# The first seven attention tiles written out by hand, and keys loaded whole from the fourth batch on

## The chip, the cores and the metric

The kernel runs on one core of a Trainium2 chip. The metric is the device time of one execution in microseconds (us). The engines are PE (matrix products), DVE (vector), ACT (scalar functions and copies), POOL (general) and SP, whose queue issues most transfers. Each works through its own instructions in order and waits on semaphores for the others.

## The reference

Three stages, each feeding the next. The inputs of the first are q, k and v of 8 batches, 8 heads, 576 positions and 64 dimensions.

```
k_p = mean of k over groups of 8 positions      # 72 pooled keys per head
v_p = mean of v over groups of 8 positions
attn = softmax(q @ k_p^T / 8)                   # per batch and head
x    = attn @ v_p                               # 4608 tokens x 512

expert = argmax over 8 experts of cos(x, expert_emb) / tau
x = gate * (relu(x @ w1[expert]) @ w2[expert])  # one expert of 8 per token

h   = max(x @ m1, x @ m2, x @ m3)               # 512 x 768 each
out = h @ m_out
```

## The kernel before, in words

The schedule is written by hand: the order of the Python calls is the order of the instructions on each engine. The attention stage handles 36 tiles of 128 tokens (4.5 per batch; tiles 4, 13, 22 and 31 hold half of one batch and half of the next), followed by the experts' products (`ph`, `py`), whose token gathers begin before the last tiles are done, and the third stage (`p`, `o`).

For one tile i there are five steps: `stage_q` transposes the queries on PE (tile `pqT`) and ACT copies them out; `stage_s` multiplies them with the pooled keys (`psc`), and DVE takes the maximum (`mx`) and subtracts it (`sh`); `stage_e` is the exponential on ACT; `stage_a` transposes the weights on PE (`paT`), two ACT copies follow (`aT`); `stage_x` multiplies with the pooled values (`pav`), and DVE scales by the reciprocal sum (`rs`, `x`), forms the expert scores (`dt`, `lg`), and SP stores x. A square sum on ACT (`sq`) is put off to a list, `squares`. Tiles 0 and 1, 2 and 3 and so on share one weights buffer, as each of the two computes four heads for both; so `stage_a(0)` needs the exponentials of tiles 0 and 1.

The loop (line 1607) runs these steps interleaved: iteration `it` calls `stage_s(it-1)`, `stage_a(it-3)`, `stage_q(it)`, `stage_e(it-1)`, the squares, `stage_x(it-4)`, then the jobs listed in `todo[it]`. PE's order is thus scores, weights transpose, query transpose, weighted values, each of another tile.

Keys and values of a batch are prepared by `prep_steps(b)` (line 297): pooling (sums of 8 rows) on DVE by one reduction per chunk (`pool_k`, `pool_v1`), or on POOL by three halvings per chunk (`pool_k2`, `pool_v`); there are five chunks of rows, four of 128 and one of 72. Then `dup_k` (ACT), transposes on PE (`ptk`, `ptv`), copies into the block-diagonal keys `kbd` (ACT), `spread_v` (POOL), and `vdot`: ten narrow matmuls (`pd`) of values with expert directions, and one DVE product. The list `at_` says at which iteration each step of a batch runs. Batches 0 to 2 are loaded whole (`load_rows`); from batch 3 on half of each row is loaded (`load_half`) and POOL later issues a transfer that adds the other half on top (`add_half`), so that pooling needs two halvings instead of three. Raw rows have two buffers each for k and v. The expert norm (`en_steps`) and constants (`const_steps`) are short DVE steps that `fill` takes from a queue between the steps of a tile.

PSUM has two rotating banks `pq` and one double bank each with the tags `psc`, `paT` and `pav`.

Of the kernel before, what the change touches and what calls it, by code (L numbers as in the profile page):

```python
# [8 lines left out]
F32 = mybir.dt.float32  # L9
# [12 lines left out]
def attention_moe_moe_kernel(  # L22
# [24 lines left out]
    nc = tc.nc  # L47
# [72 lines left out]
    if True:  # L120
# [61 lines left out]
        if True:  # L182
# [31 lines left out]
            def load_rows(pool_tag, src, b, sizes, apart=False, step=4):  # L214
                t = kvp.tile([P, 5, J, D], F32, tag=pool_tag, name=f"{pool_tag}{b}")
# [76 lines left out]
            for i in range(3):  # L292
                if i > 0:
                    nc.gpsimd.memset(kbds[i], 0.0)
                nc.gpsimd.tensor_scalar(vbds[i][:, :, D : D + 1], mslot, float(J), None, A.mult)

            def prep_steps(b):
# [9 lines left out]
                def pool_all():  # L307
                    for c in range(5):
                        pool_k(c)
# [21 lines left out]
                def spread_v():  # L331
                    for c, (h0, h1) in enumerate(HS):
# [7 lines left out]
                        )  # L340

# [67 lines left out]
                if b == 2:  # L409
                    pk = [lambda: (pool_k(0), pool_v(0, 4, P), pool_v(4, 5, R4)), *(lambda c=c: pool_k(c) for c in range(1, 5))]  # L410
# [23 lines left out]
            def stage_q(i):  # L434
# [11 lines left out]
                nc.scalar.copy(qT, ps.rearrange("p (c n) -> p c n", n=P))  # L446
                st_q[i] = qT

            def stage_s(i):
                m, part, t, segs = tiles[i]  # L450
                qT = st_q.pop(i)
                ps = pb.tile([P, 2, 512], F32, tag="psc", name=f"psc{i}")
# [63 lines left out]
            def stage_x(i):  # L516
                m, part, t, segs = tiles[i]
                aT = st_a.pop(i)
                ps = pb.tile([P, 2, 512], F32, tag="pav", name=f"pav{i}")
# [53 lines left out]

            uses = {}

            def uname(name):
                uses[name] = uses.get(name, 0) + 1
                return f"{name}_{uses[name]}"
# [926 lines left out]
            p0[0]()  # L1505
            def en_steps():
                en2 = yield from inverse_norm(ap1, ess, E, 1, "en")
                vs(en, en, en2[:, 0:1], A.mult)
                yield
                ps = pq.tile([P, 512], F32, tag="pq", name="pe0")  # L1510
# [3 lines left out]

            tok_i = rp.tile([P, NT], I32, name="tok_i")
# [71 lines left out]
            queue.append([chain(en_steps())])  # L1587
            p0[1]()
            todo = {0: [lambda: fill(16), p0[2]], 1: [lambda: fill(2), p0[3]], 2: [p0[4]], 3: [p0[5]], 5: [lambda: queue.append([chain(const_steps())])]}
# [12 lines left out]
            qnext = 3  # L1602
            kvnext = 2
# [3 lines left out]
            for it in range(NT + 4):  # L1607
# [13 lines left out]
                while qnext < len(qorder) and qorder[qnext][0] * 9 + qneed[qorder[qnext][1]] - 4 <= it:  # L1621
                    load_q(*qorder[qnext])
                    qnext += 1
                while kvnext < B and kvnext * 4.5 - 11 <= it:
                    if kvnext < NFULL:
                        kv[kvnext] = (load_rows("kraw", k, kvnext, RC), load_rows("vraw", v, kvnext, RC))
                    else:
                        kv[kvnext] = (load_half("kraw", k, kvnext), load_half("vraw", v, kvnext))
                    kvnext += 1
# [18 lines left out]
                for job in todo.get(it, []):  # L1648
                    if callable(job):
                        job()  # L1650
                        continue
                    b, j = job
                    if b not in cur:
                        cur[b] = prep_steps(b)
                    cur[b][j]()
# [351 lines left out]
```

## Time and profile before

| | |
|---|---|
| median of 3 runs | 1204.89 us (1204.51 to 1204.91) |
| profiled execution | 1203.55 us |
| its span, first to last instruction | 1201.4 us |
| PE busy | 1175.2 us (98%) |
| DVE busy | 873.2 us (73%) |
| ACT busy | 606.8 us (51%) |
| POOL busy | 297.4 us (25%) |
| granted TensorE clock, mean over the span | 0.997 |

A line of the timeline gives an instruction's start, its duration (of the whole run of xN instructions, first start to last end), engine, line in the kernel, operation, what it writes and reads, shape and count; in brackets the engine's idle time before it and what ended it. Ends of matmuls include the latency of the pipeline, so that neighbours overlap in the list.

### The profile page before, as it was taken

To read this page: it belongs to the slowest core of one execution; us is meant where nothing else is said; L and a number is where in the kernel's file an instruction comes from. 1 tells how busy PE (TensorE), PEld (TensorE's weight loads), DVE (VectorE), ACT (ScalarE), POOL (GpSimd) and SP (SyncE) were. 2 spreads that over 40 slices of the span, in tenths; PEclk is the share of its full clock that TensorE was granted. 3 is DMA by queue.
4 is the path that set the end of the run, shared out by engine and by line. 5 is a ranking of instruction groups with operands and counts; after the bars stand their busy time and mean duration, and the time that the engine had idled before them with its cause. 6 is when DMAs were issued, how large, how long until landed. Compare 5 with 4: busy or idle time off the path is not lost.

```text
span 1201.4 us, 23859 instructions
## 1 busy us (share of the span) xinstructions
PE 1175.2 (98%) x8761; PEld 1161.6 (97%) x8761; DVE 873.2 (73%) x1811; ACT 606.8 (51%) x1118; POOL 297.4 (25%) x462
## 2 busy tenths in 40 slices
PE   5999999999999999999999999999999999999997
PEld 4899999999999999999999999999999999999997
DVE  6878977978799999988765468468467557567563
ACT  4667674545666666666655244334334334334332
POOL 7978634001222122221201301103104004004001
PEclk9999999999999999999999999999999999999999
DMA  9899656328874457554939668877878877878873
GB/s 294 238 270 253 175 172 220 111 21 239 268 251 177 153 176 238 200 206 135 345 110 323 231 252 302 302 263 290 318 258 287 307 271 281 298 287 284 287 258 141
DMA packets 108121, 285.11 MB, mean 237 GB/s; under 512 B 17879, under 2 KB 70565, under 8 KB 97629
## 3 DMA queue, kind: packets, MB, share of 16 engines
q1 hardware_dynamic: 87436, 216.40, 51.8%
q0 software_dynamic: 20560, 67.11, 17.9%
q8 instruction: 71, 1.16, 0.4%
q14 instruction: 54, 0.43, 0.1%
HBM read 285.52 MB, written 52.48 MB: 281 GB/s over the span
## 4 chain that ended last, share of the span: by engine, by line
PE 92%; DVE 3%; ACT 2%; issue 1%; POOL 0%; DMA 0%; SPq 0%; POOLq 0%; DVEq 0%; ACTq 0%
PE p L1752 33%; PE ph L1097 17%; PE py L1158 17%; PE o L1864 10%; PE pav L524 3%; PE psc L470 2%; PE ph L1105 2%; PE py L1142 2%; PE px L1051 1%; PE paT L501 1%; PE pqT L445 1%; DVE sh L488 1%; DVE kp L305 1%; PE pd L379 1%; POOL out_dram L1872 0%
## 5 line engine op out<-in xcount | busy, mean ns | idle before, releaser
L1752 PE MATMUL p<-yhi,wt 128*128 128x384 f32 x1512 | 387.4, 336 | 0.1
L1752 PEld LDWEIGHTS p<-yhi,wt 128*128 128x128 f32 x1512 | 273.4, 188 | 0.3 <-issue 0.3
L1752 PE MATMUL p<-ylo,wt 128*128 128x384 f32 x756 | 254.1, 336 | 0.0
L1760 ACT COPY s<-p 128x384 f32<-128x384 f32 x162 | 77.6, 479 | 200.7 <-PE p L1752 200.7
L1158 PE MATMUL py<-hhi,whi 128*128 128x256 f32 x576 | 164.6, 286 | 0.0
L1097 PE MATMUL ph<-xhi,wlo 128*128 128x256 f32 x576 | 163.1, 283 | 0.5 <-DVE wlo L1077 0.5
L1097 PE MATMUL ph<-xhi,whi 128*128 128x256 f32 x576 | 163.5, 284 | 0.0
L1097 PE MATMUL ph<-xlo,whi 128*128 128x256 f32 x576 | 163.0, 283 | 0.0
L1158 PE MATMUL py<-hhi,wlo 128*128 128x256 f32 x576 | 162.9, 283 | 0.0
L1158 PE MATMUL py<-hlo,whi 128*128 128x256 f32 x576 | 162.9, 283 | 0.0
L1752 PEld LDWEIGHTS p<-ylo,wt 128*128 128x128 f32 x756 | 142.2, 188 | 0.0
L1864 PE MATMUL o<-wt,ghi 128*128 128x256 f32 x756 | 136.2, 282 | 0.0
L1779 DVE TENSOR_TENSOR blk<-p,s 128x384 f32<-128x384 f32 x108 | 59.6, 552 | 88.8 <-PE p L1752 88.8
L1737 POOL DMA_INDIRECT gt<-gbuf,ix x26 | 33.9, 1304 | 337.9 <-DMA ix<-idbuf 267.9
L1864 PEld LDWEIGHTS o<-wt,ghi 128*128 128x128 f32 x756 | 116.7, 188 | 0.9 <-DVE m L1780 0.8
L1097 PEld LDWEIGHTS ph<-xhi,wlo 128*128 128x128 f32 x576 | 110.5, 192 | 0.7 <-DVE wlo L1077 0.7
L1097 PEld LDWEIGHTS ph<-xhi,whi 128*128 128x128 f32 x576 | 110.5, 192 | 0.0
L1097 PEld LDWEIGHTS ph<-xlo,whi 128*128 128x128 f32 x576 | 110.5, 192 | 0.0
L1158 PEld LDWEIGHTS py<-hlo,whi 128*128 128x128 f32 x576 | 110.5, 192 | 0.0
L1158 PEld LDWEIGHTS py<-hhi,whi 128*128 128x128 f32 x576 | 110.4, 192 | 0.0
L1158 PEld LDWEIGHTS py<-hhi,wlo 128*128 128x128 f32 x576 | 110.4, 192 | 0.0
L1077 DVE TENSOR_TENSOR wlo<-w2raw,whi 128x1024 fp32r<-128x1024 f32 x86 | 105.1, 1225 | 6.9 <-ACT whi L1068 6.8
(345 smaller groups left out, 2348.6 us busy)
## 6 DMA issues: line engine op xcount, KB each, us to landing
wt<-wdram SPq DMA_DIRECT2D x69, 1792.0 KB
w1raw<-in_moe_w_dram SPq DMA_DIRECT2D x88, 512.0 KB
w2raw<-in_moe_w_dram SPq DMA_DIRECT2D x88, 512.0 KB
wdram<-wst POOLq DMA_DIRECT2D x9, 1792.0 KB, 6.6
ybuf<-yo SPq DMA_DIRECT2D x40, 256.0 KB
cvraw<-in_moe_w_dram POOLq DMA_DIRECT2D x36, 256.0 KB, 4.4
xbuf<-x SPq DMA_DIRECT2D x16, 512.0 KB
yr<-ybuf SPq DMA_DIRECT2D x20, 384.0 KB
```

The lines of the kernel that those rows point to most:

```text
L470: nc.tensor.matmul(ps[:, c // 2, (c % 2) * 2 * SP : (c % 2 + 1) * 2 * SP], qT[:, c, :], kbds[segs[0][2] % 3][:, h0 + c].rearrange("p t s - ...
L524: nc.tensor.matmul(ps[lo:hi, bank, (g0 % 4) * DA : (g0 % 4 + g1 - g0) * DA], aT[:, c, lo:hi], vbds[b % 3][:, sl : sl + g1 - g0, :].rearran ...
L1077: nc.vector.tensor_tensor(lo, src, hi.bitcast(F32), op=A.subtract)
L1097: nc.tensor.matmul(ps[:, f, :], a_[:, c, fs], b_[:, c, :], start=(n == 0), stop=(n == 3 * DC - 1))
L1105: nc.tensor.matmul(ps[:, f, 0:P], tl["w1"][piece][:, c, fs], xlo[:, c, 0:P], start=(c == 0), stop=(c == DC - 1))
L1142: nc.tensor.matmul(ps[h], a_[:, f, 0:P], b_[:, f, cols], start=(piece == 0 and f == 0 and n == 0), stop=(last_ and f == 1 and n == 2),)
L1158: nc.tensor.matmul(py[:, c // 2, (c % 2) * 256 : (c % 2 + 1) * 256], a_[:, f, c * P : (c + 1) * P], b_[:, f, :], start=(piece == 0 and f = ...
L1737: nc.gpsimd.indirect_dma_start(out=gt[g][:, j : j + 1], out_offset=None, in_=gbuf[:, :], in_offset=bass.IndirectOffsetOnAxis(ap=cols[j], a ...
L1752: nc.tensor.matmul(ps, a_, b_, start=(start and c + n == 0), stop=(c == 1 and n == 2), skip_group_check=True)
L1760: nc.scalar.copy(t, ps)
L1779: tt(src, add[0], add[1], op=A.add)
L1864: nc.tensor.matmul(ps, a_, b_, start=(m in (1, 2, 5) and c + n == 0), stop=(c == KH - 1 and n == 2), skip_group_check=True,)
```

## The change

Buffers of raw rows get a tag per parity of the batch, one buffer each. Keys are loaded whole in every batch, so POOL's pooling of keys always takes three halvings; values from batch 3 on still come by halves. Loads of batch 1 move up by one query load. Before the first keys come, `turn(22)` issues 22 products of the identity with itself, and `turn(3)` and `turn(12)` stand later; their result is not used. Two chunks of batch 0's keys go from DVE to POOL, and the expert norm runs on DVE between the other three. The iterations 0 to 7 of the loop are replaced by a list of calls, with scores of tiles 0 to 2 in other PSUM tags; the loop begins at iteration 8. Steps of batch 2 move to iterations 8 to 10, the pooling of batch 3 from iteration 6 to 9, the constants from 5 to 11.

```
             def load_rows(pool_tag, src, b, sizes, apart=False, step=4):
-                t = kvp.tile([P, 5, J, D], F32, tag=pool_tag, name=f"{pool_tag}{b}")
+                t = kvp.tile([P, 5, J, D], F32, tag=f"{pool_tag}{b % 2}", name=f"{pool_tag}{b}_", bufs=1)
...
+            kv[1] = [load_rows("kraw", k, 1, RC)]
             load_q(0, 1)
-            kv[1] = [load_rows("kraw", k, 1, RC)]
+            kv[1].append(load_rows("vraw", v, 1, RC))
             load_q(0, 2)
-            kv[1].append(load_rows("vraw", v, 1, RC))
...
+            def later_blocks(i0, i1):
+                for i in range(i0, i1):
                     nc.gpsimd.memset(kbds[i], 0.0)
+                    nc.gpsimd.tensor_scalar(vbds[i][:, :, D : D + 1], mslot, float(J), None, A.mult)
+            def turn(n):
+                ps = pb.tile([P, 2, 512], F32, tag="pav", name=uname("turn"))
+                for _ in range(n):
+                    nc.tensor.matmul(ps[:, 0, 0:P], ident, ident, start=True, stop=True)
...
-                def pool_all():
-                    for c in range(5):
+                def pool_one(c):
+                    n = RC[c]
+                    for w in (4, 2, 1):
+                        dst = kt[0:n, c, 0:w, :] if w > 1 else kp[0:n, c, 0:1, :]
+                        nc.gpsimd.tensor_tensor(dst, kt[0:n, c, 0:w, :], kt[0:n, c, w : 2 * w, :], op=A.add)
+                def pool_all(between):
+                    pool_one(1)
+                    pool_one(4)
+                    for c, n in ((0, 5), (2, 11), (3, 0)):
+                        for _ in range(n):
+                            next(between, None)
                         pool_k(c)
...
-                        for w in (4, 2, 1) if b < NFULL else (2, 1):
+                        for w in (4, 2, 1):
...
+                def trans_k0():
+                    for tag, c0, c1, h0, h1 in (("paT", 0, 4, 0, 7), ("psc", 4, 5, 7, 8)):
...
                 if b == 0:
                     return [
-                        lambda: (pool_all(), dup_k(), trans_k(range(4), 0, 7), trans_k([4], 7, 8)),
-                        lambda: (pool_v(2, 4, P), pool_v(4, 5, R4)),
-                        lambda: pool_v1(0),
-                        lambda: (pool_v1(1), spread_v()),
+                        lambda between: (pool_all(between), dup_k(), trans_k0()),
+                        lambda: pool_v(2, 4, P),
+                        lambda: (pool_v1(0), pool_v1(1), pool_v1(4), spread_v((2, 3, 0, 1, 4))),
                         lambda: (trans_v(0, 4), trans_v(4, 5)),
-                        lambda: vdot(),
+                        vdot,
                     ]
                 if b == 1:
                     return [
-                        lambda: (pool_k(0), pool_k(1), pool_k2(RC, 2), pool_v(0, 4, P), pool_v(4, 5, R4)),
-                        lambda: (dup_k(), spread_v(), trans_k(range(4), 0, 7), trans_k([4], 7, 8)),
+                        lambda: (pool_k(0), pool_k(1)),
+                        lambda: (pool_k2(RC, 2), pool_v(0, 4, P), pool_v(4, 5, R4), spread_v()),
+                        dup_k,
+                        lambda: (trans_k(range(4), 0, 7), trans_k([4], 7, 8)),
                         lambda: (trans_v(4, 5), trans_v(0, 4)),
                         vdot,
                     ]
                 if b == 2:
-                    pk = [lambda: (pool_k(0), pool_v(0, 4, P), pool_v(4, 5, R4)), *(lambda c=c: pool_k(c) for c in range(1, 5))]
+                    pk = [lambda: (pool_v(0, 4, P), pool_v(4, 5, R4))]
+                    pk += [lambda c0=c0: [pool_k(c) for c in range(c0, min(c0 + 2, 5))] for c0 in (0, 2, 4)]
                     return pk + [spread_v, lambda: trans_kv(range(4), 0), lambda: trans_kv([4], 4 * P), vdot]
...
-                at_ = {1: [2, 4, 6, 7], 2: [5, 6, 6, 7, 7, 7, 8, 9, 10]}.get(b, at_[:4] + at_[5:6])
+                at_ = {1: [], 2: [None, None, 8, 8, 9, 9, 9, 10], 3: [9, 10, 12, 13, 14]}.get(b, at_[:4] + at_[5:6])
                 if b >= NFULL:
-                    todo.setdefault(need - 9, []).append(
-                        lambda b=b: (add_half(k, b, kv[b][0]), add_half(v, b, kv[b][1]))
+                    todo.setdefault(8 if b == 3 else need - 9, []).append(
+                        lambda b=b: add_half(v, b, kv[b][1])
                     )
...
+            turn(22)
+            en_left = en_steps()
+            p0[0](en_left)
...
+            later_blocks(1, 2)
             p0[1]()
...
+            load_kv(2)
+            for _ in en_left:
+                pass
+            stage_q(0)
+            stage_q(2)
+            turn(3)
+            stage_s(0)
+            stage_s(2)
+            en_products()
+            p0[2]()
+            later_blocks(2, 3)
+            turn(12)
+            stage_e(0)
+            stage_e(2)
+            stage_q(1)
+            stage_q(3)
+            stage_s(1)
+            p0[3]()
+            stage_s(3)
+            stage_e(1)
+            p0[4]()
+            stage_a(0)
+            stage_e(3)
+            p1 = prep_steps(1)
+            p1[0]()
+            p1[1]()
+            stage_x(0)
+            stage_a(1)
+            stage_x(1)
+            stage_q(4)
+            stage_a(2)
+            p1[2]()
+            p1[3]()
+            stage_x(2)
+            kv[3] = [load_rows("kraw", k, 3, RC)]
+            load_q(1, 0)
+            stage_a(3)
+            stage_s(4)
+            stage_q(5)
+            sq_rest()
+            stage_x(3)
+            stage_s(5)
+            stage_e(4)
+            sq_rest()
+            stage_a(4)
+            stage_q(6)
+            cur[2] = prep_steps(2)
+            cur[2][1]()
+            kv[3].append(load_half("vraw", v, 3))
+            stage_s(6)
+            stage_e(5)
+            p1[4]()
+            cur[2][0]()
+            p1[5]()
+            stage_q(7)
+            stage_e(6)
+            for it in range(8, NT + 4):
```

## Rows read from the trace of the kernel before

**Rows 1.** The page's engines: busy us, share of the span, instructions.
```profile
PE 1175.2 (98%) x8761; PEld 1161.6 (97%) x8761; DVE 873.2 (73%) x1811; ACT 606.8 (51%) x1118; POOL 297.4 (25%) x462
```
**Rows 2.** The chain of waits that ended last, share of the span by engine.
```profile
PE 92%; DVE 3%; ACT 2%; issue 1%; POOL 0%; DMA 0%; SPq 0%; POOLq 0%; DVEq 0%; ACTq 0%
```
**Rows 3.** Timeline, the start: start us, us, engine, line, operation, count, idle before.
```profile
7.37 2.88 DVE L305 TENSOR_REDUCE kp<-kraw 128x64 f32<-128x512 f32 x3 [1.25 <-DMA kraw<-in_k_dram]
...
9.89 1.19 PE L347 MATMUL ptk<-ident,kp 128*128 128x128 f32 x5 [9.89 <-ACT kp L323]
```
**Rows 4.** Timeline of PE, first tiles.
```profile
12.27 1.11 PE L445 MATMUL pqT<-ident,qgrp 128*128 128x128 f32 x4 [1.19 <-ACT kbd L352]
...
18.65 2.29 PE L470 MATMUL psc<-kbd,qT 128*128 128x144 f32 x8 [0.67 <-ACT qT L446]
...
22.72 1.15 PE L470 MATMUL psc<-kbd,qT 128*128 128x144 f32 x8
```
**Rows 5.** Timeline of PE, later: one of each kind, and the waits.
```profile
23.71 0.71 PE L501 MATMUL paT<-ident,at 128*128 128x128 f32 x5
24.25 0.60 PE L445 MATMUL pqT<-ident,qgrp 128*128 128x128 f32 x4
24.69 1.18 PE L379 MATMUL pd<-enT,vT 128*128 128x16 f32 x10
...
28.17 1.69 PE L524 MATMUL pav<-vbd,aT 128*128 128x146 f32 x12
...
32.00 1.19 PE L456 MATMUL psc<-kbd,qT 128*64 128x144 f32 x14 [0.79 <-ACT kbd L352]
...
46.20 1.95 PE L470 MATMUL psc<-kbd,qT 128*128 128x144 f32 x8 [1.05 <-DVE sh L488]
...
56.27 1.25 PE L470 MATMUL psc<-kbd,qT 128*128 128x144 f32 x8 [0.29 <-ACT qT L446]
```
**Rows 6.** Busy time by stretch: PE, PEld, DVE, ACT, POOL, granted clock, DMA share, GB/s.
```profile
46.00:48.00 2.00, 1.80 (x9) 1.82 (x10) 2.00 (x12) 1.30 (x3) 1.76 (x5) 0.63 1.22 199
```
**Rows 7.** Timeline of all engines: steps of DVE and ACT around a tile.
```profile
28.25 0.76 DVE L488 TENSOR_TENSOR sh<-psc,mx 128x576 f32<-128x576 f32 x1
...
29.64 0.55 ACT L323 COPY kp<-kp 128x256 f32<-128x256 f32 x2
...
35.88 0.17 DVE L534 TENSOR_SCALAR rs<-pav 128x8 f32<-128x8 f32 x1 [1.02 <-PE pav L524]
...
37.18 0.28 DVE L551 TENSOR_REDUCE lg<-dt 128x8 f32<-128x64 f32 x1
...
37.51 0.58 ACT L503 COPY aT<-paT 128x512 f32<-128x512 f32 x1 [1.11 <-PE paT L501]
...
37.99 0.26 ACT L504 COPY aT<-paT 72x128 f32<-72x128 f32 x1
38.15 0.59 ACT L446 COPY qT<-pqT 128x512 f32<-128x512 f32 x1
...
48.50 1.98 DVE L305 TENSOR_REDUCE kp<-kraw 128x64 f32<-128x512 f32 x2
...
52.04 0.68 ACT L494 ACTIVATE at<-sh 128x576 f32<-128x576 f32 x1 [1.34 <-DVE sh L488]
...
52.63 0.61 ACT L557 ACTIVATE sq<-x 128x512 f32<-128x512 f32 x1
...
53.24 0.56 ACT L365 COPY kbd<-ptk 64x504 f32<-64x504 f32 x1
```
**Rows 8.** Timeline of POOL: halvings of whole and half rows, and transfers it issues.
```profile
28.62 1.26 POOL L329 TENSOR_TENSOR vraw<-vraw 128x256 f32<-128x256 f32 x2
...
29.96 0.32 POOL L329 TENSOR_TENSOR vp<-vraw 128x64 f32<-128x64 f32 x1
...
37.56 2.38 POOL L212 DMA_DIRECT2D kraw<-in_k_dram  x2 [0.56 <-DVE lg L551]
...
50.31 0.45 POOL L319 TENSOR_TENSOR kraw<-kraw 128x128 f32<-128x128 f32 x1
```

More of the change, by code (lines that the diff above doesn't have):

```diff
@@ L214, in load_rows @@
             def load_rows(pool_tag, src, b, sizes, apart=False, step=4):
-                t = kvp.tile([P, 5, J, D], F32, tag=pool_tag, name=f"{pool_tag}{b}")
+                t = kvp.tile([P, 5, J, D], F32, tag=f"{pool_tag}{b % 2}", name=f"{pool_tag}{b}_", bufs=1)
                 flat = src[b].rearrange("h (s j) d -> (h s) (j d)", j=J)
@@ L329, in pool_v, with spread_v @@
                             nc.gpsimd.tensor_tensor(dst, vt[0:n, c, 0:w, :], vt[0:n, c, w : 2 * w, :], op=A.add)
-                def spread_v():
-                    for c, (h0, h1) in enumerate(HS):
+                def spread_v(order=range(5)):
+                    for c in order:
+                        h0, h1 = HS[c]
                         n = RC[c]
@@ L340, in spread_v @@
                         )
+                def trans_k0():
+                    for tag, c0, c1, h0, h1 in (("paT", 0, 4, 0, 7), ("psc", 4, 5, 7, 8)):
+                        ps = pb.tile([P, 2 * 512], F32, tag=tag, name=f"ptk0_{h0}")
+                        for c in range(c0, c1):
+                            n = KC[c]
+                            nc.tensor.transpose(
+                                ps[:, (c - c0) * P : (c - c0) * P + n],
+                                kp[0:n, c].rearrange("p two d -> p (two d)"),
+                                ident[0:n, 0:n],
+                            )
+                        n = (h1 - h0) * SP
+                        nc.scalar.copy(kb[0:D, h0:h1, 0, :], ps[0:D, 0:n].rearrange("p (h s) -> p h s", s=SP))
+                        nc.scalar.copy(kb[D:P, h0:h1, 1, :], ps[D:P, 0:n].rearrange("p (h s) -> p h s", s=SP))
                 def trans_k(cs, h0, h1):
@@ L445, in stage_q @@
                     nc.tensor.transpose(ps[:, c * P : (c + 1) * P], blk_, ident)
-                nc.scalar.copy(qT, ps.rearrange("p (c n) -> p c n", n=P))
+                copy = nc.vector.tensor_copy if i == 0 else nc.scalar.copy
+                copy(qT, ps.rearrange("p (c n) -> p c n", n=P))
                 st_q[i] = qT
@@ L451, in stage_s @@
                 qT = st_q.pop(i)
-                ps = pb.tile([P, 2, 512], F32, tag="psc", name=f"psc{i}")
+                ps = pb.tile([P, 2, 512], F32, tag={1: "pav", 2: "paT"}.get(i, "psc"), name=f"psc{i}")
                 if part == 1:
@@ L518, in stage_x @@
                 aT = st_a.pop(i)
-                ps = pb.tile([P, 2, 512], F32, tag="pav", name=f"pav{i}")
+                ps = pb.tile([P, 2, 512], F32, tag="psc" if i == 1 else "pav", name=f"pav{i}")
                 for bank in range(2):
@@ L1504, in attention_moe_moe_kernel @@
             nc.scalar.activation(esq, en, AF.Square, accum_out=ess)
-            p0[0]()
             def en_steps():
@@ L1509, in en_steps, with en_products @@
                 yield
+            def en_products():
                 ps = pq.tile([P, 512], F32, tag="pq", name="pe0")
@@ L1585, in const_steps @@
                 yield
-            queue.append([chain(en_steps())])
+            later_blocks(1, 2)
             p0[1]()
-            todo = {0: [lambda: fill(16), p0[2]], 1: [lambda: fill(2), p0[3]], 2: [p0[4]], 3: [p0[5]], 5: [lambda: queue.append([chain(const_steps())])]}
+            todo = {11: [lambda: queue.append([chain(const_steps())])]}
             for b in range(1, B):
@@ L1601, in attention_moe_moe_kernel @@
             qneed = {0: 0, 1: 4, 2: 5}
-            qnext = 3
-            kvnext = 2
             cur = {}
@@ L1606, in attention_moe_moe_kernel, with load_kv, loads @@
             first = run(range(NREQ), between)
-            for it in range(NT + 4):
+            def load_kv(n):
+                kv[n] = (
+                    load_rows("kraw", k, n, RC),
+                    load_rows("vraw", v, n, RC) if n < NFULL else load_half("vraw", v, n),
+                )
+            def loads(it):
+                while counts[0] < len(qorder) and qorder[counts[0]][0] * 9 + qneed[qorder[counts[0]][1]] - 4 <= it:
+                    load_q(*qorder[counts[0]])
+                    counts[0] += 1
+                while counts[1] < B and max(counts[1] * 4.5 - 11, 9) <= it:
+                    load_kv(counts[1])
+                    counts[1] += 1
@@ new lines, in jobs, with sq_rest @@
+            def jobs(it):
+                for job in todo.get(it, []):
+                    if callable(job):
+                        job()
+                        continue
+                    b, j = job
+                    if b not in cur:
+                        cur[b] = prep_steps(b)
+                    cur[b][j]()
+            def sq_rest():
+                while squares:
+                    squares.pop()()
+            counts = [4, 4]
+            load_kv(2)
+            for _ in en_left:
+                pass
@@ L1620, in attention_moe_moe_kernel @@
                     open_b()
[L1621 to L1629, printed above, removed]
+                loads(it)
                 if 0 <= it - 1 < NT:
@@ L1647, in attention_moe_moe_kernel @@
                     next(first)
[L1648 to L1655, printed above, removed]
+                jobs(it)
                 if it == NT - 1 and started:
```

12 lines of the change are left out of this document (5 added, 7 removed).

## The prediction, made before the changed kernel was run

> **What bounds the kernel now.** I read the share table first: PE is busy 98% of the span [rows 1], and the chain of waits that ended last is 92% PE [rows 2]. So any microsecond that PE loses or gains early is carried to the end, unless a later wait takes it up. The change touches the first seven of the 36 token tiles and the pooling of keys, so the PE timeline up to tile 9 decides. There the reader is to see three things.
>
> First, PE starts late: its first instruction comes at 9.89 us, behind DVE's key reductions, which waited for the load of batch 0's keys until 7.37 [rows 3]. Second, it starts at half pace: four query transposes took 1.11 us at 12.27 and eight score matmuls 2.29 at 18.65, but 1.15 for the same eight at 22.72 [rows 4] and 0.60 for four transposes at 24.25 [rows 5]. That is 1.2 against 2.4 GHz, although the view of the clock has no entry for the beginning. Third, there is a dip: PE idled 1.05 us before the scores of tile 7 at 46.20, waiting for DVE [rows 5], and the granted clock of the next 2 us is 0.63 [rows 6]. After that PE is almost without gaps, so I compare the start of tile 9's scores (56.27, [rows 5]): all PE work ahead of it is the same in both kernels, but for the added `turn` matmuls, and from there on the order of PE is the same.
>
> **The pace of PE.** Ends in the rows include the pipeline's latency, so I take start to start: scores 1.03, transpose of the attention weights (paT) 0.55, query transpose 0.44, weighted values (pav) 1.52, value dot (pd) 1.07 us (each duration in [rows 5] less some 0.16 of latency). One tile is 3.54 us.
>
> **The change, part by part.**
>
> *Warm-up.* `turn(22)` needs only the identity and fills PE from about 1.6 us on: 22 x 0.22 at half pace (a fourth of 0.44, doubled) is 4.9 us, over by 6.5. It lies ahead of the first key transpose and hides behind the key load, so it costs nothing. Whether it buys anything depends on the clock surviving the 3 idle us until 9.89. A gap of 1.05 was enough for a dip at 46.20, so I assume that PE is at half pace again. From 9.89 on PE is then without a gap (5 + 4 + 4 transposes, `turn(3)`, two score groups). In the kernel before the pace doubled 4.1 us into the first such stretch (18.65 to 22.72), so I take full pace from 15; the ends are 9.9 and 18.
>
> *Start of keys.* DVE does three key chunks instead of five, with the norm of the experts in its idle time, POOL the other two; but the third and fourth chunk still come after the landing at 7.37, two reductions of 1 us, then the copies. PE starts at 9.9 as before: nothing gained or lost here, except that some 4 us of DVE work are gone from the time behind it. If POOL's chunk 4 lands late, up to 1 us is lost.
>
> *The hand-made order.* In the loop before, a tile's four PE parts stand in four different iterations, so each copy by ACT is covered by PE work of other tiles. By hand `stage_a(0); stage_x(0)`, `stage_a(1); stage_x(1)` and `stage_q(7); stage_s(7)` stand next to each other. PE then waits for ACT: paT's latency 0.17, the two copies 0.58 and 0.26 [rows 7] and about 0.1 for signals, 1.08 us; behind a query transpose 0.17 + 0.59 + 0.15 = 0.95. Full sequence, starting with tile 1's scores. Their query copy stands on ACT behind the exponentials of tiles 0 and 2, which wait for DVE: scores 0 end at 15.4 (9.9 + 1.1 + 2 x 0.88 + 0.66 + 2.06, all at half pace), four DVE steps of 0.76 [rows 7] with 0.02 between them give 18.55, two exponentials and the copy, some 1.2, so 19.75. Then
> - scores 1, transpose of v, scores 3, pd: 3.75, to 23.5;
> - twice paT, wait, pav: 2 x (0.55 + 1.08 + 1.52) = 6.3, to 29.8;
> - query 4, paT 2, wait, keys' transpose, pav 2: 0.44 + 0.55 + 1.41 + 0.55 + 1.52, to 34.3; the wait is two copies and the doubling of keys, 0.55 [rows 7];
> - paT 3, scores 4 (1.27), query 5, pav 3, scores 5: 4.8, to 39.1;
> - paT 4 waits 1.12 (ACT does three squares of 0.6 [rows 7] ahead of the exponential of tile 4), query 6, wait 1.15, scores 6, transpose of v, wait 0.95, pd, query 7, wait 0.95: 8.25 together, to 47.35.
>
> Scores 7 start at 47.35 instead of 46.20: 1.1 us later, although the cold stretch is some 7 us shorter. The seven waits after 19.75 sum to 7.7 us.
>
> *Keys of batch 2.* Their last three reductions and their transposes move to iterations 8 and 9 (transposes: before, iteration 8 for the first four chunks). Scores 9 need the copies of these keys. PE goes on from 47.35 with 3.54 us up to the end of pav 4 (51.0 with latency). DVE, in order: results of tile 4, 1.5 (35.88 to 37.46 [rows 7]); three reductions, 2.9 (1.98 for two [rows 7]); maximum and subtraction of tile 8, 1.55: 57.0. ACT, in order: exponential 0.68, square 0.6, two key copies of 0.56 [rows 7], with signals: 59.3. PE has scores 8, paT 6, query 9, pav 5 and the transposes, all done by 55.8. It idles some 3.6 us. Scores 9 start at 59.3 against 56.27: 3.0 us later.
>
> *The dip.* The dip after 46.20 cost before: 2 us at 0.63 and some more, about 1.7 us, and is in the 56.27. A 1.05 us wait with narrow pd matmuls ahead of it was enough for it; the 3.6 us wait ahead of scores 9 should bring another, then behind the point of comparison: +1.7 (0 if the clock holds, 3.4 if it takes twice as long).
>
> *Whole keys.* Per batch from the fourth on, POOL adds a first halving: a chunk takes 1.6 (1.26 + 0.32 [rows 8]) instead of 0.8 (two steps, 0.45 the first [rows 8]), so 4 us more for five; it loses the issue of the accumulating key transfer, 2.4 [rows 8]. Net +1.6 us of POOL per batch. A batch needs 4.5 x 3.54 + 2.2 = 18 us of PE, and POOL's 12 us of pooling fit in; so I take 0. Without that cover it is 1.6 per batch, 8 us in all.
>
> *The rest.* Raw buffers by even and odd batch are the same two buffers in the same turn: 0. Loads of batch 1 move ahead of two query loads, each needed later: 0, 1 us at most. The constants on DVE move from iteration 5 to 11, where DVE waits for PE: 0 (that they are gone from iterations 5 to 8 is in the sum).
>
> **Sum.** +3.0 and +1.7: 4.7 us. The profiled execution took 1203.55 (span 1201.4, 2.15 around it), so 1208.2; the median of the runs lies 1.34 above the profiled one, so 1209.6.
>
> **Rivals.**
> 1. *The clock swings through the whole hand-made stretch.* For: PE idles half of 39 to 47 (4.2 of 8.25), and [rows 6] shows what a shorter wait did. Against: PE waited 0.79 at 32.00 [rows 5] and full pace stayed. Two more dips, 3.4 us: 1213. The Trainium skill, page "TensorE: Matmul & The Clock Gate", section "A second HAM failure mode: psum-queue depth-cycling", says that frequent micro-idles between groups of matmuls make the clock swing between its levels; by that rule this rival would be the forecast, and the dip at 46.20 agrees with it, while the stretch up to 46 does not.
> 2. *The warm-up holds.* PE at full pace from 9.9: the cold 5 us shrink by half, -2.3, and no second dip: 59.3 - 2.3 - 56.3 = +0.7, so 1205.6, no change. Against: the idle time from 6.5 to 9.9.
> 3. *Faster.* PE's own work from 9.9 to scores 7 is only about 26 us at full pace, so without waits scores 7 could start at 38. The place that decides is the chain DVE-ACT behind each score group: if copies overlap with PE (each matmul waiting only for its own chunk, ACT less queued), half of the 12 us of waits from 18 to 59 (0.9 ahead of scores 1, 7.7, 3.6) go, -6, with the dip still there: -1.3; with the warm-up holding too, -3.6: 1201.3. It decides from 4.7 us of waits fewer than I count. For: the waits are worked out, not seen.
> 4. *POOL becomes the bound* with whole keys: +4 to +8 on top, 1215. Against: the 12 of 18 us.
>
> **Chances.** Forecast 0.44, rival 1 0.13, rival 2 0.17, rival 3 0.21, rival 4 0.05. A measurement tells about 0.2% (2.4 us) from no change. Slower: forecast, rivals 1 and 4, 0.62; same: 0.17; faster: 0.21. The likeliest case's own range is 1207 to 1212; the range that leaves out no more than 0.2 reaches from 1200.5 to 1215.
>
> **What would show it.** Right: a wait of some 3 us on PE ahead of tile 9's scores, released by ACT's key copy; waits of about 1 us ahead of pav 0, pav 1 and scores 7; scores 7 between 46 and 49; a clock below 1 behind 59. Wrong: scores 9 before 56, PE without gaps between 23 and 47, or the first key transposes at full pace. If PE waits for POOL's pooled keys from tile 13 on, rival 4.

## The result, and the profile after

The changed kernel takes 1214.62 us (median of 4 runs, 1213.40 to 1215.04), the kernel before 1204.90 beside it: ratio 1.0077, 95% interval 1.0061 to 1.0093. It is slower by 9.7 us, twice the forecast of 4.7. The profiled execution took 1213.40 (span 1211.7).

The page of the changed kernel: its engines, and the chain that ended last.

```profile
PE 1184.1 (98%) x8835; PEld 1169.3 (97%) x8835; DVE 881.8 (73%) x1811; ACT 607.1 (50%) x1117; POOL 310.8 (26%) x480
...
PE 89%; DVE 6%; ACT 2%; issue 1%; DMA 1%; POOL 0%; POOLq 0%; DVEq 0%; ACTq 0%
```

PE still bounds it, but DVE's part of the chain doubled from the 3% of [rows 2], and POOL is busy 13 us longer than in [rows 1] (it pools whole keys now). Where PE now waits, from its timeline (start us, us, engine, line, operation, count, idle time before and its releaser):

```profile
1.46 8.03 PE L309 MATMUL turn<-ident 128*128 128x128 f32 x44 [1.46 <-POOL ident masks.py:199]
10.76 0.72 PE L372 MATMUL ptk<-ident,kp 128*128 128x128 f32 x5 [1.27 <-ACT kp L347]
...
24.79 1.76 PE L566 MATMUL pav<-vbd,aT 128*128 128x146 f32 x12 [0.72 <-ACT aT L545]
...
27.77 1.79 PE L566 MATMUL pav<-vbd,aT 128*128 128x146 f32 x12 [0.68 <-ACT aT L545]
...
31.73 0.72 PE L386 MATMUL ptk<-ident,kp 128*128 128x128 f32 x5 [1.19 <-ACT kp L347]
...
39.66 0.76 PE L543 MATMUL paT<-ident,atm 128*128 128x128 f32 x5 [0.83 <-ACT atm L536]
...
41.74 1.25 PE L512 MATMUL psc<-kbd,qT 128*128 128x144 f32 x8 [0.88 <-ACT qT L488]
...
44.20 1.28 PE L418 MATMUL pd<-enT,vT 128*128 128x16 f32 x10 [0.67 <-ACT vT L413]
...
46.65 1.25 PE L512 MATMUL psc<-kbd,qT 128*128 128x144 f32 x8 [0.68 <-ACT qT L488]
...
58.87 2.29 PE L512 MATMUL psc<-kbd,qT 128*128 128x144 f32 x8 [3.51 <-ACT kbd L405]
...
65.10 1.23 PE L512 MATMUL psc<-kbd,qT 128*128 128x144 f32 x8
...
87.17 1.22 PE L512 MATMUL psc<-kbd,qT 128*128 128x144 f32 x8 [0.56 <-DVE sh L530]
...
107.97 1.76 PE L566 MATMUL pav<-vbd,aT 128*128 128x146 f32 x12 [0.67 <-DVE dt L591]
...
110.72 1.22 PE L512 MATMUL psc<-kbd,qT 128*128 128x144 f32 x8 [0.99 <-DVE rs L576]
...
124.21 1.22 PE L512 MATMUL psc<-kbd,qT 128*128 128x144 f32 x8 [0.42 <-DVE pre L617]
```

The reader is to see three stretches. Up to tile 7, ACT's hand-offs. Then 3.51 us ahead of tile 9's scores (58.87; 56.27 in [rows 5]), and behind them these scores at half pace, 2.29. The view of stretches shows why (PE, PEld, DVE, ACT, POOL busy; granted clock; DMA share; GB/s):

```profile
58.00:60.00 2.00, 1.13 (x5) 1.13 (x6) 0.00 (x0) 1.92 (x6) 1.83 (x5) 0.67 0.97 343
60.00:62.00 2.00, 2.00 (x10) 1.96 (x10) 0.76 (x1) 0.11 (x1) 1.76 (x6) 0.50 1.07 316
```

And last, from 75 to 125 us (from the weighted values of tile 9 on), eight waits of 0.25 to 0.99 us for DVE; the kernel before has none of that length for DVE between 58 and 125. The first two are the forecast's. To size the third, I take in each kernel the start of the weighted values (pav) of tiles 3, 8 and 28. From tile 8 to tile 28 PE has the same matmuls, by tile and count, in all of them, so what the distance grows by against the kernel before is time lost there (last column). Ahead of tile 3 the work is not the same: the hand-made order has this pav ahead of scores 5 and 6, a paT, two query transposes and a transpose of v that the loop has run by then, 4.0 us at the prediction's paces. So the column of tile 3 compares only kernels of the same order.

| kernel (edit against its parent) | tile 3 | tile 8 | tile 28 | lost from 8 to 28 |
|---|---|---|---|---|
| before | 42.30 | 66.52 | 153.21 | 0 |
| after | 36.11 | 70.68 | 162.64 | 5.3 |
| e1: after, keys by halves | 37.10 | 71.54 | 159.62 | 1.4 |
| e2: before, whole keys | 41.77 | 68.20 | 156.79 | 1.9 |
| e3: after, constants at iteration 8 | 37.09 | 74.10 | 163.78 | 3.0 |
| e4: after, no turn(22) | 37.47 | 73.77 | 166.12 | 5.7 |
| e5: after, early keys of batch 2 | 35.61 | 64.55 | 157.32 | 6.1 |
| e6: after, constants by hand | 35.80 | 71.58 | 161.29 | 3.0 |
| e7: e1, e5 and e6 together | 37.26 | 66.06 | 153.51 | 0.8 |
| e8: before, with turn(22) | 41.40 | 66.51 | 153.19 | 0.0 |
| e9: after, no first halving | 35.80 | 72.07 | 159.54 | 0.8 |
| e10: after, no spreading | 35.79 | 71.94 | 160.86 | 2.2 |
| e11: e7, reordered | 35.06 | 64.26 | 153.07 | 2.1 |
| e12: e11, POOL's jobs moved | 34.34 | 64.20 | 151.55 | 0.7 |

Of the 6.2 us by which the changed kernel's pav 3 comes earlier, some 4 are thus order and some 2 a lead. At scores 7, where PE has the same work behind it in both but for the `turn` products, it is 0.45 behind (46.65 against 46.20); it is 4.2 behind at tile 8, 9.4 at tile 28, and 0.9 more comes in the rest of the span. The 5.3 us from 8 to 28 are what no term of the forecast holds. Each row is one profiled execution: these lie between 1.4 us below their kernel's median and 2.2 above it (e2).

Which DVE steps grew there? Groups by line and shape, DVE, 58 to 150 us (count, busy us, mean ns of one, idle before), first the kernel before, then the changed one:

```profile
L488 DVE TENSOR_TENSOR sh<-psc,mx 128x576 f32<-128x576 f32 x22 | 16.6, 755 | 1.3
...
L590 DVE SCALAR_TENSOR_TENSOR wt<-lg,w 128x72 f32<-128x72 f32 x2 | 0.7, 362 | 0.1
...
L593 DVE TENSOR_REDUCE wm<-wt 128x9 f32<-128x72 f32 x2 | 0.5, 229 | 0.0
L581 DVE TENSOR_TENSOR rk<-cnt,prk 128x72 f32<-128x72 f32 x2 | 0.4, 222 | 0.0
L651 DVE COPY pre<-oh 128x72 f32<-128x72 f32 x2 | 0.4, 187 | 0.0
```

```profile
L530 DVE TENSOR_TENSOR sh<-psc,mx 128x576 f32<-128x576 f32 x20 | 15.1, 754 | 1.1
...
L626 DVE SCALAR_TENSOR_TENSOR wt<-lg,w 128x72 f32<-128x72 f32 x2 | 2.2, 1079 | 0.0
L687 DVE COPY pre<-oh 128x72 f32<-128x72 f32 x2 | 2.0, 980 | 0.0
...
L617 DVE TENSOR_TENSOR rk<-cnt,prk 128x72 f32<-128x72 f32 x2 | 0.4, 222 | 0.0
L629 DVE TENSOR_REDUCE wm<-wt 128x9 f32<-128x72 f32 x2 | 0.4, 221 | 0.0
```

The steps wt, wm, oh, pre, rk, slot and ohs are the rank steps: they find each token's expert and its place in that expert's list, for several tiles at once. Steps that read PSUM (sh, rk from prk) and reductions are unchanged. Of the copies and element-wise steps with all operands in SBUF the two worst are shown, three and five times as long in the mean (wt, pre from oh); the others grow by factors of up to 2.3, and the reciprocal rs<-rs not at all (198 and 195 ns). Beside one of them stands POOL, at work without a pause (timeline of DVE and POOL, changed kernel):

```profile
119.36 0.68 DVE L586 TENSOR_TENSOR x<-pav,rs 128x512 f32<-128x512 f32 x1
119.53 2.81 POOL L360 TENSOR_TENSOR vbd<-kp,mslot 128x128 f32<-128x128 f32 x5
...
120.55 1.67 DVE L687 COPY pre<-oh 128x72 f32<-128x72 f32 x1
121.44 1.66 POOL L343 TENSOR_TENSOR kraw__1554<-kraw__1554 128x256 f32<-128x256 f32 x1
```

A copy of 0.19 us takes 1.67 while POOL spreads values and goes straight on to the next batch's first halving. Between 50 and 160 us every stretched DVE step of either kernel lies beside POOL's work, but not every such step beside POOL is stretched: of the eight steps pre<-pre 128x72 of the changed kernel, all beside POOL, five are. In the kernel before POOL stands idle four times over 1 us between 58 and 145 us, for 4.8, 2.3, 1.6 and 2.6 us (three times for a transfer, once for PE's key transposes); two of these:

```profile
71.45 0.45 POOL L319 TENSOR_TENSOR kraw<-kraw 128x128 f32<-128x128 f32 x1 [4.76 <-DMA kraw<-in_k_dram]
...
105.98 0.46 POOL L319 TENSOR_TENSOR kraw<-kraw 128x128 f32<-128x128 f32 x1 [1.62 <-PE ptk L359]
```

In the changed kernel one is left there (5.7 us, up to 118.15). And in the kernel before the spreading at 83, 100 and 119 us falls where DVE has only a tile's own steps, none of which is stretched.

Theory 1: whole keys fill POOL's pauses, DVE's small steps beside it are stretched, and DVE makes PE wait. Theory 2: the constants, moved from iteration 5 to 11, crowd DVE where the rank steps begin.

### The profile page after: what moved, and what is told of

Same layout as the page of the kernel before. It is cut to its first block, busy times and chain, and to the rows that moved or that the text cites. A ratio compares the mean times of both kernels' runs of the same rounds, so it can differ in the third digit from the quotient of the medians.

```text
span 1211.7 us, 24019 instructions
## 1 busy us (share of the span) xinstructions
PE 1184.1 (98%) x8835; PEld 1169.3 (97%) x8835; DVE 881.8 (73%) x1811; ACT 607.1 (50%) x1117; POOL 310.8 (26%) x480
## 4 chain that ended last, share of the span: by engine, by line
PE 89%; DVE 6%; ACT 2%; issue 1%; DMA 1%; POOL 0%; POOLq 0%; DVEq 0%; ACTq 0%
PE p L1862 32%; PE ph L1133 16%; PE py L1194 16%; PE o L1974 10%; PE pav L566 3%; PE psc L512 2%; PE ph L1141 2%; PE py L1178 2%; PE px L1087 1%; PE paT L543 1%; PE pqT L486 1%; DMA cvraw<-in_moe_w_dram 1%; DVE sh L530 1%; DVE x L586 1%; DVE mx L527 0%
## 5 line engine op out<-in xcount | busy, mean ns | idle before, releaser
L1847 POOL DMA_INDIRECT gt<-gbuf,ix x26 | 36.7, 1412 | 335.9 <-DMA ix<-idbuf 329.5
```

The lines of the kernel that those rows point to most:

```text
L1847: nc.gpsimd.indirect_dma_start(out=gt[g][:, j : j + 1], out_offset=None, in_=gbuf[:, :], in_offset=bass.IndirectOffsetOnAxis(ap=cols[j], a ...
```

## The experiments

Each was timed in 5 rounds beside the kernel before, whose medians in the four groups were 1205.0 to 1206.4, with single runs from 1202.7 to 1207.6; so differences below some 1.5 us are not settled by the times. Ratios are against before. The diffs show the lines that matter.

**e1, keys by halves.** In the changed kernel:

```diff
-  load_rows("kraw", k, n, RC),
+  load_rows("kraw", k, n, RC) if n < NFULL else load_half("kraw", k, n),
-  lambda b=b: add_half(v, b, kv[b][1])
+  lambda b=b: (add_half(k, b, kv[b][0]), add_half(v, b, kv[b][1]))
-  kv[3] = [load_rows("kraw", k, 3, RC)]
+  kv[3] = [load_half("kraw", k, 3)]
-  for w in (4, 2, 1):
+  for w in (4, 2, 1) if b < NFULL else (2, 1):
```

> The changed kernel, but keys of batches 3 to 7 again loaded by halves, the second half accumulated by POOL's transfer, with two halvings instead of three. Theory 1: the third halving leaves POOL without pauses between 50 and 137 us, small DVE steps beside it are stretched, and DVE makes PE wait in tiles 13 to 28; that cost 5.3 us, so the time falls from 1214.6 by 4 to 5 us to 1210, and the rank steps are back at 0.2 to 0.4 us (wt 128x72 mean near 0.36 us instead of 1.08). Theory 2 (the constants, moved from iteration 5 to 11, push the rank steps late and crowd DVE): within 1 us of 1214.6. Scores 9 stay at 58.9 under both.

Measured 1210.79, ratio 1.0045 (1.0032 to 1.0058): 3.8 us back, just under the 4 to 5 of theory 1; lost from tile 8 to 28: 1.4 instead of 5.3. POOL's pauses are back (2.5 us at 86, 2.7 at 109), wt is at 322 ns, though pre<-oh only at 686.

**e2, whole keys alone**, in the kernel before:

```diff
-  kv[kvnext] = (load_half("kraw", k, kvnext), load_half("vraw", v, kvnext))
+  kv[kvnext] = (load_rows("kraw", k, kvnext, RC), load_half("vraw", v, kvnext))
-  lambda b=b: (add_half(k, b, kv[b][0]), add_half(v, b, kv[b][1]))
+  lambda b=b: add_half(v, b, kv[b][1])
-  for w in (4, 2, 1) if b < NFULL else (2, 1):
+  for w in (4, 2, 1):
```

> The kernel before, with one part of the change alone: keys of batches 3 to 7 loaded whole, three halvings on POOL, no accumulating transfer for them. Theory 1: 4 to 5 us slower than before, 1209 to 1210, with PE waiting for DVE between tiles 13 and 28 and scores 9 unmoved at 56.3. Theory 2: no change, 1204 to 1206.

Measured 1205.26, ratio 1.0002 (0.9993 to 1.0011): no change, theory 1's number is missed. Its profiled execution took 1207.45, 2.2 us more than this median. In that trace POOL runs without a pause too, and steps are stretched (wt 639 ns), but between tiles 8 and 28 only two waits of 1.1 and 0.9 us for DVE reach PE (at 98.33 and 136.66). Ahead of tile 8 it waits twice at key transposes, once for POOL's pooled values:

```profile
52.62 0.33 PE L359 MATMUL ptk<-ident,kp 128*128 128x128 f32 x1 [1.29 <-POOL kp L329]
...
98.33 1.76 PE L524 MATMUL pav<-vbd,aT 128*128 128x146 f32 x12 [1.08 <-DVE dt L549]
```

So, if theory 1 holds, whole keys cost only where POOL's runs meet the wrong DVE steps, and in the order before they mostly don't. This condition is argued, not shown; e9 and e10 test the theory in the new order.

**e3, constants at iteration 8, and e6, by hand.**

```diff
-  todo = {11: [lambda: queue.append([chain(const_steps())])]}
+  todo = {8: [lambda: queue.append([chain(const_steps())])]}     # e3
+  todo = {}                                                      # e6
   stage_x(1)
+  for _ in const_steps(): pass                                   # e6
   stage_q(4)
```

> The changed kernel, with the constants queued at iteration 8 instead of 11. Theory 2: DVE is done with them before the first rank steps, the waits for DVE in tiles 13 to 21 go, 3 to 4 us faster: 1211. Theory 1: less than 1 us either way on that stretch; the constants then stand beside the key reductions of batch 2, so scores 9 may come up to 1 us later: 1214 to 1216.

> The changed kernel, with all steps of the constants run in one go in DVE's idle time behind tile 1's results (2.9 us idle at 31 to 34) instead of the queue from iteration 11. If the constants' place made the waits for DVE in tiles 13 to 28 (theory 2): 3 to 4 us faster, 1211. If POOL's longer halvings did (theory 1): 1 us or less, 1213.5 to 1215. If both are needed, DVE having too little slack for the constants and the stretching together: 3 us, as the halves alone gave 3.8.

Measured 1214.68 (1.0075, 1.0061 to 1.0089) and 1214.13 (1.0077, 1.0063 to 1.0091): no gain, theory 2 falls as the cause of the time. In the traces the constants do have a part: lost from 8 to 28 are 3.0 us in both, not 5.3. Tile by tile, nothing is lost up to tile 14 (2.7 in the changed kernel), but 3.0 and 2.4 at tile 15, where the changed kernel loses nothing: part of the loss only moves. And as e1 takes away 3.9 of the 5.3 and the constants 2.3, the two overlap; their shares can't be told apart. In e3 the rest had been lost earlier (7.6 behind at tile 8, after half pace behind scores 9 from 60 to 66 us); in e6 that half pace lasted longer too, from 58 to 64.

**e4, no turn(22)**: the line `turn(22)` removed.

> The changed kernel without turn(22), the 44 passes over the identity before the first key transposes; turn(3) and turn(12) stay. If the clock stays up through the 1.27 us between them and the keys (what the trace of the changed kernel reads like), the first transposes and scores are then at half pace again, for about 4 us of full-pace work: scores 1 come some 2 us later, scores 9 by at most that since DVE sets them, so 1214.6 plus 0 to 2.5. If the warm-up had bought nothing, no change.

Measured 1216.41 (1.0088, 1.0075 to 1.0101), 1.8 us more; the intervals of e4 and of the changed kernel overlap. In the trace the first key transposes take 1.22 instead of 0.72.

**e5, early keys of batch 2.**

```diff
-  2: [None, None, 8, 8, 9, 9, 9, 10]
+  2: [None, None, None, None, 9, 8, 8, 10]
   p1[5]()
+  cur[2][2]()
+  cur[2][3]()
   stage_q(7)
```

> The changed kernel, with the last three key reductions of batch 2 put into DVE's idle time behind iteration 7's query transposes (2.16 us idle at 45.8) and this batch's key transposes in iteration 8 instead of 9. Forecast's theory (the chain reductions, maximum, exponential, key copies sets scores 9): the 3.5 us wait ahead of scores 9 goes, with it the dip, scores 9 at about 55 and scores 10 near 60 instead of 65.1; the time falls by 4 to 5 us to 1210. Rival (the wait only moves: DVE is late for the next tile, or the clock dips at another place): 1213 to 1215.

Measured 1209.47 (1.0044, 1.0030 to 1.0058): 5.1 us less. Tile 9's scores come without a wait and at full pace, so the forecast's chain was the cause of this loss. The same trace shows POOL's run at its worst (timeline, PE, DVE, POOL):

```profile
54.35 1.19 PE L512 MATMUL psc<-kbd,qT 128*128 128x144 f32 x8
...
97.32 3.18 DVE L726 TENSOR_SCALAR ohs<-iof,slot,tokid 128x128 f16<-128x128 f32 x2
97.53 2.84 POOL L360 TENSOR_TENSOR vbd<-kp,mslot 128x128 f32<-128x128 f32 x5
...
102.36 1.76 PE L566 MATMUL pav<-vbd,aT 128*128 128x146 f32 x12 [2.58 <-DVE dt L591]
```

Of the two steps of DVE in the first row, 0.39 us each in the kernel before (its mean of 18), one took 2.93 and ended at 100.25, as POOL's spreading ended (100.37), and PE then waited 2.58.

**e9, no first halving, and e10, no spreading for batches 4 to 7**, in the changed kernel:

```diff
-  for w in (4, 2, 1):
+  for w in (4, 2, 1) if b < NFULL else (2, 1):       # e9
-  spread_v,
+  spread_v if b == 3 else lambda: None,              # e10
```

> The changed kernel with the keys of batches 3 to 7 loaded whole, but POOL leaves out the first of the three halvings (so these keys are sums over half of their rows; the order and the loads stay). Theory 1 (POOL's work beside DVE's small steps): the same gain as the halves gave, 3 to 4.5 us, 1210 to 1211.5, and the rank steps near 0.2 to 0.4 us. Rival (the loads: whole keys through SP's queue land later, or crowd the queue): 1213.5 to 1215, no gain.

> The changed kernel, but POOL leaves out the spreading of the pooled values for batches 4 to 7 (2.8 us each; tiles of these batches then use the values of an earlier batch). In the trace of the changed kernel the longest stretched DVE steps (wt 1.72 at 82.11, rk 1.40 at 98.75, pre 1.67 at 120.55) lie beside this spreading. If it is POOL's runs without a gap that hold DVE up, whichever instruction they are made of: the stretched steps shrink to 0.2 to 0.5 us, 2 to 4.5 us faster, 1210 to 1212.5. If only the first halvings do it: less than 1 us, 1214.

Measured 1213.41 (1.0065, 1.0050 to 1.0080) and 1213.16 (1.0056, 1.0040 to 1.0072). By their medians they gain 1.2 and 1.5 us, by their ratios 1.4 and 2.5 (the kernel before was 1.5 us slower beside them than beside the changed kernel): less than theory 1 asked for. But both change the values, and with them which expert a token goes to; the expert stages behind tile 35 do other work (from there to the last `ph` matmuls e9 loses 2.1 us, the changed kernel 0.6). So I read only the stretch from 8 to 28. There e9 loses 0.8 instead of 5.3, with the loads as in the changed kernel: 4.5 of the 5.3 hang on POOL's first halvings, not on the transfers. e10 loses 2.2: the spreading is part of the run that holds DVE up. e9 still has pre<-oh at 334 ns, e10 wt at 642.

**e7, three edits together** (e1, e5, e6).

> The changed kernel with three edits together: keys of batches 3 to 7 by halves, early reductions and transposes for batch 2, the constants in DVE's idle time at 31 us. If the three losses are separate they add: 1214.6 less 3.8 (measured for the halves), less 4 to 5, less up to 1: 1205 to 1207, the time of the kernel before. If the hand-made stretch then keeps the 6 us that it is ahead at tile 3, 1201 to 1203 and faster than both.

Measured 1205.30 (1.0002, 0.9990 to 1.0015). By medians the three were worth 3.8, 5.1 and 0.5; together 9.3 (by ratios 3.9, 4.0 and 0; together 9.0). So, within this noise, the 9.7 us are accounted for: 4 to 5 for the keys of batch 2, some 4 for whole keys. The 6 us that the expectation hoped to keep were mostly order, as said below the table: scores 7 come at 47.65 in e7, 1.45 behind the kernel before. One of these microseconds went at the start. View of stretches of e7:

```profile
8.00:10.00 2.00, 0.06 (x1) 0.00 (x0) 1.91 (x3) 0.00 (x0) 1.43 (x3) 1.00 1.02 383
10.00:12.00 2.00, 1.54 (x11) 1.54 (x12) 0.17 (x1) 1.39 (x4) 1.89 (x18) 0.82 1.07 351
12.00:14.00 2.00, 2.00 (x12) 2.00 (x11) 0.53 (x1) 1.32 (x4) 1.80 (x5) 0.50 1.08 315
```

Here turn(22) took 6.60 us, 2.40 us of idle time followed, and the clock fell to 0.50 behind it. In the changed kernel turn(22) took 8.03, the gap was 1.27, and no stretch up to 58 is below 1.00. The code is the same up to there: how long turn(22) takes, and so the gap behind it, differs from run to run.

**e8, the warm-up alone**: turn(22) ahead of the key pooling in the kernel before.

> The kernel before, with turn(22) alone added ahead of the first key transposes. If a warm PE is worth something by itself: the first transposes and scores take half their time (0.6 instead of 1.1 for four query transposes, 1.15 instead of 2.3 for eight score matmuls); about 5 us less of PE work up to 22.7, of which the waits for DVE and ACT take a part back: 1201 to 1204. In the changed kernel turn(22) was worth 1.8 us (1216.4 without it), which would make 1203. If the waits take it all back: 1205.

Measured 1205.10 (1.0001, 0.9992 to 1.0010): nothing. PE's timeline says why:

```profile
9.24 1.06 PE L347 MATMUL ptk<-ident,kp 128*128 128x128 f32 x5 [0.40 <-ACT kp L323]
...
17.36 2.29 PE L470 MATMUL psc<-kbd,qT 128*128 128x144 f32 x8 [0.68 <-ACT qT L446]
...
48.68 1.56 PE L524 MATMUL pav<-vbd,aT 128*64 128x146 f32 x22 [0.72 <-DVE vbd L386]
...
52.14 1.22 PE L470 MATMUL psc<-kbd,qT 128*128 128x144 f32 x8 [1.30 <-DVE rs L534]
```

The clock was up at 10 but fell at 12.9, among waits of 0.4 to 0.9 us, and was 0.50 until 23.2. What was won, up to 2.5 us ahead at tile 4, DVE took back at 45 to 52; tile 9's scores stand at 56.26, against 56.27.

**e11, reordered by hand.** e7 with turn(26), the constants in two parts, and in short:

```diff
-  stage_a(0); stage_x(0); stage_a(1); stage_x(1); stage_q(4); stage_a(2)
+  stage_a(0); stage_q(4); stage_x(0); stage_a(1); stage_q(5); stage_x(1); stage_a(2)
...
-  stage_s(5); stage_e(4); sq_rest(); stage_a(4); stage_q(6)
+  stage_e(4); stage_s(5); stage_a(4); stage_q(6); sq_rest()
...
-  stage_s(6); p1[4](); p1[5](); stage_q(7)
+  p1[4](); stage_s(6); stage_q(7); p1[5]()
```

> The kernel with early keys of batch 2, halves and early constants (1205.3), with turn(26) for turn(22), and the hand-made order changed so that each query or value transpose stands between a transpose and the product that waits for ACT's copy of it; the constants in two parts; squares behind the copies. If ACT's hand-offs (0.72, 0.67, 1.2, 0.35, 0.88, 0.67, 0.67, some 5 us) are what the hand-made stretch loses: tile 7's scores at 43 to 45 instead of 47.6, 1201.5 to 1203.5 and faster than the kernel before. If DVE and POOL set the pace there (DVE has some 12 us idle of 24 to 50 before): the waits move to DVE, 1204 to 1206. turn(26) should keep the clock at full pace from the keys on in each run; in the trace with the three edits it fell to 0.5 from 11 to 15.

Measured 1204.97 (0.9993, 0.9983 to 1.0003): tile 7's scores at 44.81, 2.2 us ahead from tile 6 to 24, then nothing left. The trace of e11 and the clock behind it:

```profile
134.04 3.08 POOL L1745 DMA_DIRECT2D ybuf<-ones  x4
...
134.88 0.77 DVE L687 COPY pre<-oh 128x48 f32<-128x48 f32 x1
...
137.37 0.36 PE L697 MATMUL prk<-pre,ones 128*128 128x8 f32 x2 [1.66 <-DVE pre L617]
```

```profile
138.00:142.00 4.00, 4.00 (x20) 3.98 (x20) 2.18 (x6) 1.29 (x3) 1.06 (x4) 0.59 0.52 201
```

**e12, POOL's jobs moved**, in e11: the output's fill (POOL's issue of four transfers to `ybuf`) at `it == MA + 2`, two iterations later, and the spreading of batch 7 in iteration 31 instead of 28.

> The reordered kernel (1204.97), with two of POOL's jobs put behind the third rank chain: the issue of the output's fill (3.08 us on POOL) two iterations later, and the spreading of batch 7's values in iteration 31 instead of 28. In the trace of the reordered kernel these stand beside that chain: pre<-oh 128x48 took 0.77 instead of 0.19, PE waited 1.66 for it at 137.37 and ran the next 2.4 us at about half pace, so the 2.2 us won by then were gone. If POOL beside DVE's small steps made that wait: pre<-oh 128x48 at 0.2 us again, the wait at 1 us or less, the 2.2 us kept: 1202.5 to 1204. If the chain is late for another reason: the wait stays and the time with it, 1204.5 to 1206.

Measured 1204.59 (0.9994, 0.9984 to 1.0004). In its trace the steps are short again and the wait is the usual one:

```profile
131.68 3.09 POOL L1746 DMA_DIRECT2D ybuf<-ones  x4
...
134.54 0.21 DVE L617 TENSOR_TENSOR oh<-w,wm 128x48 f32<-128x48 f32 x1
...
134.78 0.19 DVE L687 COPY pre<-oh 128x48 f32<-128x48 f32 x1
...
137.08 0.39 PE L697 MATMUL prk<-pre,ones 128*128 128x8 f32 x2 [0.88 <-ACT qT L488]
```

1.6 us are kept to tile 35. POOL's pooling ended 2.4 us earlier in this run, so the fill comes at 131.7 instead of 134.0, and no spreading follows it. This does not settle what held DVE up in e11: there oh (0.42 us), pre<-oh (0.77) and pre<-pre (0.57) lay beside the fill, while here lg, wt and oh lie beside the same fill and take 0.21 each. Nor is it shown that each move was needed. The median is 1.3 us below that of before, but the interval holds 1: no version is shown to beat the kernel before.

## Why the prediction was right and wrong

- **Warm-up: wrong on the clock, small in effect.** 22 products stand in the trace as 44 matmul records and took 8.0 us, not 4.9. The clock stayed up through the gap, as rival 2 had it, and the first key transposes ran at full pace (0.72 us), which the prediction had named as a sign of being wrong; what that is worth is 1.8 us (e4), not settled by the intervals.
- **Start of keys: nothing lost, wrong by 0.9.** The keys come at 10.76 instead of 9.89 [rows 3]: between the landing and the last two reductions stands the last expert-norm step, and it took 0.97 us instead of 0.47, beside POOL's new halvings. In this trace the mechanism that I missed later stands here already; in e1, e3, e5 and e7 the same step took 0.47 or 0.48, and the keys came at 10.25 to 10.46.
- **Scores 1: right by luck.** Forecast 19.75, found 19.67, by another path. The exponentials were done at 18.12, about 1 us earlier than counted, and then ACT waited for the query transposes, which stand on PE behind `turn(12)`; the forecast's sum has `turn(12)` nowhere, and no run leaves it out.

```profile
15.62 2.94 PE L309 MATMUL turn<-ident 128*128 128x128 f32 x24
...
19.04 1.08 ACT L488 COPY qT<-pqT 128x512 f32<-128x512 f32 x2 [0.92 <-PE pqT L486]
```

- **Hand-offs: right, somewhat large.** The seven waits counted as 7.7 us are 5.7 (0.72, 0.68, 1.19, 0.83, 0.88, 0.67, 0.68): each is 0.2 to 0.4 shorter than counted. (Two of the working's sums are off by 0.03 and 0.04: its terms give 1.11 and 0.91, not 1.08 and 0.95.) Scores 7 at 46.65; forecast 47.35, before 46.20.
- **Keys of batch 2: right.** Wait 3.6 forecast, 3.51 found; scores 9 at 59.3 forecast, 58.87 found; e5 takes the wait away and 5.1 us with it.
- **The dip: right.** +1.7 forecast; tile 9 to tile 10 the delay grows from 2.6 to 4.15, so +1.55, at a granted 0.50. Sum up to there: 4.7 forecast, 4.2 found, with the errors above partly cancelling. Tile 10's scores in the kernel before:

```profile
60.95 1.23 PE L470 MATMUL psc<-kbd,qT 128*128 128x144 f32 x8
```

- **Whole keys and constants at 0: this step failed.** "POOL's 12 us of pooling fit in" was true and beside the point. In the changed kernel PE never waits for POOL's pooled keys; the price is paid on DVE, where some of the small steps stand still while POOL runs without a pause. It is 3.8 us by e1's time and 4 to 4.5 of the 5.3 us by the traces of e1 and e9. I wrote "without that cover it is 1.6 per batch, 8 us in all", and the range held 1214.6 through rival 4's number, but rival 4's sign (PE waiting for POOL's keys) did not come: as to these 5 us the range held by luck. I asked whether POOL has time, not what POOL's work does to the engine beside it. The constants alone, moved, change the time by 0.5 us or less.
- Rival 1, a clock that swings through the hand-made stretch, came in part: the trace of the changed kernel has seven waits there and 1.00 from 24 to 58, but of the seven experiments with the same order up to tile 7 (e1, e3 to e6, e9, e10) three show 0.50 for a while between 46 and 52 (e4, e9, e10), which goes with the 1.4 and 1.3 us that e9 and e10 are further behind at tile 8. In e8 waits of 0.4 to 0.9 us brought it down too. The rule of the Trainium skill that I weighed (page "TensorE: Matmul & The Clock Gate", section "A second HAM failure mode: psum-queue depth-cycling") agrees with these four and not with the other five.

Left open: why whole keys cost 3.8 us in the new order and nothing measurable in the old one. Added up over the single DVE steps between 58 and 150 us that took over 1.3 times the shortest of their kind, the excess is 2.1 us in the kernel before, 9.7 in the changed one, 5.7 in e1, 3.1 in e9 and 6.2 in e2: DVE is held up in the old order too, but less. The traces show that other DVE steps lie beside POOL's runs; that this alone makes the difference was not tried by moving POOL's runs in e2. And what is won early comes back later in e8 and e11, so some of the 9.7 us may depend on phase, not on any one part.

## What to carry to other kernels

Cost added work on one engine not only by whether that engine has time, but by what its neighbours do meanwhile; here POOL's extra halvings were hidden for POOL and paid on DVE. When an order is written by hand, follow each batch's whole preparation to its first use: the 1.8 us by which tile 5's weighted values came earlier were 4.2 us of delay one tile later, behind one late key copy. A mark compares two orders only where the same work lies ahead of it. Undo the parts one by one and then together, to see whether the losses add up.

## What the runs showed of the hardware

DVE's copies, casts and element-wise steps with all operands in SBUF took up to nine times as long beside POOL's uninterrupted runs (0.19 to 1.67 us), though not each time, while reductions (221 ns), the reciprocal (195 ns) and steps that read PSUM (sh 754, rk from prk 222 ns) did not change. The Trainium skill, page "SBUF — State Buffer", section "🔬 SBUF: two separate sides", says that DVE and GpSimd share one pair of ports under an exclusive lock, which a DVE step in a 2-port mode needs, or one with two SBUF inputs against a GpSimd instruction that reads SBUF, and that the loser fully blocks for the whole instruction. The rows agree on who is hit. On how long they go further: POOL's spreading is five instructions in 2.8 us, and while the DVE copy stood from 120.55 to 122.21, three more instructions of POOL started (120.83, 121.19, 121.44).

After the warm-up the granted clock fell to 0.50 behind idle gaps of 2.21, 2.25 and 2.40 us (e1, e3, e7) and stayed at 1.00 behind 1.27, 1.40, 1.62 and 1.99 (the changed kernel and e6, e5, e9, e10); each kernel was profiled once.
